# Combine softmax of all six chunks in one pass in the middle, running maximum as a logit column, w1 loads begun earlier, another memory order for w2

## The chip, the core and the metric

One core of a Trainium2 chip runs the whole program. Its engines are PE (TensorE: matmuls, with a separate stream PEld for weight loads), DVE (VectorE), ACT (ScalarE), POOL (GpSimd) and SP (SyncE, which here only issues DMAs). Each engine runs its instructions in the order in which the program has them, and waits for semaphores of the others. The metric is the device time of one execution in microseconds (us); the kernel before is timed three times and the median counts.

## The reference, cut to what matters

```python
# 1. gated recurrence per batch b (4) and head h (8), 768 tokens, head size 40
for t in range(S):
    m_new = maximum(f + m, i);  f_stab = exp(f + m - m_new);  i_stab = exp(i - m_new)
    C = f_stab * C + i_stab * outer(v, k);  n = f_stab * n + i_stab * k
    y[:, :, t] = sigmoid(o_gate) * (C @ q) / maximum(abs(n . q), 1)
x = y as 3072 tokens x 320
# 2. soft mixture of experts: 8 experts x 4 slots = 32 slots
logits = x @ phi                                   # 3072 x 32
d = softmax over the tokens of logits              # "dispatch", one maximum per slot
slot_input = d.T @ x                               # 32 x 320
for e in range(8): slot_out[e] = relu(slot_input[e] @ w1[e]) @ w2[e]
c = exp(logits - logits.max(1)); c /= c.sum(1) + 1e-9    # "combine", one maximum per token
x = c @ slot_out
# 3. h = x @ w_in; h * softmax(h), normalised, times g_ln, @ w_out   -> 3072 x 320
```

w_in and w_out arrive as 64-bit floats and are decoded on the chip.

## The kernel before

The work has three stages in one program.

**The recurrence.** A unit is 128 tokens of one batch, for all 8 heads: unit i = 4c + b is chunk c (of 6) of batch b (of 4). A loop runs over the 24 units; one pass of four units is called a cycle here. What a unit needs is a set of small closures, `ops(i)`, keyed by names, and the table `ORDER[i % 4]` gives the order in which the names are emitted: work of unit i (the output matmuls `o0` to `o3` into `po` and `pr`, the state updates `u0` to `u3` into `dps`), of unit i - 1 (`numa`, `numb`: DVE lines L296 and L298 build the numerator `num`; `den0` to `den2`: L306, L308, L310 the denominator `rd`; `sg`: L314; `x`: the product on POOL, L329, into a tile x; `C`: L325), of unit i - 2 (`xT`: the transpose of x) and of units i + 1 and i + 2 (`scA`, `scB` scores; `wA`, `wB`: DVE L253; `R`, `exp`: gate matrices). Since each engine keeps the order of emission, `ORDER` sets what stands behind what. `ENG` says which operations run on POOL; there, beside L329, run `cd` (L285), `kw` (L238) and `D4` (L457), a part of the decoding of w_in and w_out, which is spread over the loop too (DVE L446 to L455).

**Logits inside the loop.** Once per cycle the logits of a finished chunk g are made: `lt` multiplies phi by the four transposed x, so that `lt_t` has 4 batches x 32 slots on the 128 partitions and 128 tokens along the columns. For the dispatch softmax DVE takes the negated maximum per row (`tm0`, L360); `tm1` (L364) takes the minimum with that of the chunk before, which makes a running maximum; `tm2` exponentiates on ACT. `nt` and `ntc` (L379) bring the exponentials and the logits back to tokens on partitions, in the tile `dn` of 256 columns; `sl` and `acc` add up the slot inputs.

**The combine softmax, per chunk.** `row0` to `row7` run on the 128 logit columns of `dn`, spread over the cycle after: maximum (DVE L388), subtraction (POOL L390), exponential (ACT L392), sum (DVE L394), + 1e-9 (L396), reciprocal (L398), product (L400), two casts to the high part (L404), two subtractions for the low part (POOL L407). `cTp` (PE, four transposes) and `cTc` (ACT L430) put the result into `cT`. For the last chunk these steps run in the tail, all of those on DVE and POOL there on DVE.

**The middle.** After the loop follow the last unit's logits and sums, the slots' inputs `sbd`, then the expert layers: `w1_mm` (PE L761) in two column halves of 20 matmuls each, 512 columns wide (the trace shows two records for one such matmul); `hidden(0)` (ACT L754) and the four transposes `hT` (L766) of the first half stand ahead of the last 8 matmuls of the second. Then `cTp` of the last chunk, and `w2_mm` (L802) over the eight experts' w2 in the order 0, 2, 4, 6, 1, 3, 5, 7; then `soT`, `swc`, `sw_ps`, small steps that multiply the slots' output by w_in. `keep_warm` are matmuls whose result nobody uses.

**The last stage**, 24 tiles of 128 tokens through the layer of part 3, is a software pipeline with a table of its own.

**Loads.** SP issues every DMA in program order. A DMA also waits for the one that was issued eight before it, since there are eight semaphores. The 20 tiles of w1 (512 KB each) go one per unit from i = 4 to 22, the last at i = 22 too; the eight w2 (1280 KB each) follow, into memory that other tiles held, so that each waits for the last reader of these:

```python
W1_AT = 4
...
    for i in range(NU):
        ...
        if W1_AT <= i < W1_AT + 19:
            SP.dma_start(out=w1s[:, i - W1_AT, :], in_=w1p[i - W1_AT])
```

Of the kernel before, what the change touches and what calls it, by code (L numbers as in the profile page):

```python
# [45 lines left out]
def tile_kernel(  # L46
# [335 lines left out]
    def row_soft(g, k):  # L382
        nat = GR[g]["dn"][:, 128:256].rearrange("p (j s) -> p j s", j=NB)
        if k == 0:
            GR[g]["rs"] = rs_t
        rs = GR[g]["rs"]
        if k == 0:
            V.tensor_reduce(out=rs[:, 0, :], in_=nat, axis=AX.X, op=ALU.max)  # L388
# [640 lines left out]
```

## Time and profile before

| | us |
|---|---|
| times of three runs | 323.53, 321.88, 318.48 |
| median | 321.88 |
| the profiled execution | 319.83 |
| its span, first to last instruction | 318.0 |
| PE busy in the span | 297.0 |
| DVE busy | 253.1 |
| ACT busy | 213.8 |
| POOL busy | 74.5 |

The span is what the trace shows; 1.83 us of the profiled execution lie around it. Busy time of an engine holds time in which an instruction has begun and stands still, so that a busy engine need not be at its peak. By stages, the first logits' maximum (L360) starts at 51.2 us and the fifth at 147.2, the expert layers begin at 167.5, and the last stage runs from 194.9 to the end.

### The profile page before, as it was taken

To read this page: it belongs to the slowest core of one execution; us is meant where nothing else is said; L and a number is where in the kernel's file an instruction comes from. 1 tells how busy PE (TensorE), PEld (TensorE's weight loads), DVE (VectorE), ACT (ScalarE), POOL (GpSimd) and SP (SyncE) were. 2 spreads that over 40 slices of the span, in tenths; PEclk is the share of its full clock that TensorE was granted. 3 is DMA by queue.
4 is the path that set the end of the run, shared out by engine and by line. 5 is a ranking of instruction groups with operands and counts; after the bars stand their busy time and mean duration, and the time that the engine had idled before them with its cause. 6 is when DMAs were issued, how large, how long until landed. Compare 5 with 4: busy or idle time off the path is not lost.

```text
span 318.0 us, 8486 instructions
## 1 busy us (share of the span) xinstructions
PE 297.0 (93%) x3345; PEld 236.6 (74%) x3345; DVE 253.1 (80%) x568; ACT 213.8 (67%) x458; POOL 74.5 (23%) x107
## 2 busy tenths in 40 slices
PE   8985998999988998989999997999999999999995
PEld 5554676767766766767653335899999999999995
DVE  8688699899999999999827135988887787887841
ACT  5375676676666765857721604698988988988983
POOL 4412065465466365354300000000000000000000
PEclk9997899999999999999999999999999999999999
DMA  6961779788878798789999600011011010010111
GB/s 169 304 126 31 250 247 286 233 301 275 275 270 265 251 291 275 247 310 324 366 363 362 206 11 0 0 44 38 25 41 43 21 44 31 33 43 21 43 41 41
DMA packets 26086, 52.06 MB, mean 164 GB/s; under 512 B 3904, under 2 KB 15872, under 8 KB 26048
## 3 DMA queue, kind: packets, MB, share of 16 engines
q1 hardware_dynamic: 26048, 51.53, 50.3%
q8 instruction: 26, 0.43, 0.6%
q14 instruction: 12, 0.10, 0.1%
HBM read 47.03 MB, written 3.93 MB: 160 GB/s over the span
## 4 chain that ended last, share of the span: by engine, by line
PE 65%; DVE 19%; DMA 7%; ACT 3%; issue 3%; POOL 2%; POOLq 0%; DVEq 0%; ACTq 0%; SPq 0%
PE o L916 9%; PE o L918 9%; PE o L917 9%; PE uT L901 7%; PE h L857 4%; PE po L267 3%; PE sc L249 3%; DVE lb L253 3%; PE R L217 2%; PE R L218 2%; DMA w2s<-w 2%; DMA w1s<-w1p 2%; PE pr L270 2%; DMA gr<-m 2%; DVE kvo L314 2%
## 5 line engine op out<-in xcount | busy, mean ns | idle before, releaser
L916 PE MATMUL o<-wh,uh 128*128 128x320 f32 x192 | 62.9, 328 | 0.0
L918 PE MATMUL o<-wh,ul 128*128 128x320 f32 x192 | 59.1, 308 | 0.0
L917 PE MATMUL o<-wl,uh 128*128 128x320 f32 x192 | 59.0, 308 | 0.0
L876 DVE SCALAR_TENSOR_TENSOR u<-h,e 128x1024 f32<-128x1024 f32 (+1 forms) x25 | 29.4, 1181 | 16.8 <-ACT e L869 16.8
L267 PE MATMUL po<-kvo,lb 128*64 128x41 f32 x768 | 38.1, 230 | 3.3 <-PE sc L249 2.0
L267 PEld LDWEIGHTS po<-kvo,lb 128*64 128x64 f32 x768 | 30.7, 139 | 9.9 <-issue 4.8
L917 PEld LDWEIGHTS o<-wl,uh 128*128 128x128 f32 x192 | 36.2, 188 | 0.9
L916 PEld LDWEIGHTS o<-wh,uh 128*128 128x128 f32 x192 | 36.1, 188 | 0.9
L918 PEld LDWEIGHTS o<-wh,ul 128*128 128x128 f32 x192 | 36.0, 187 | 0.0
L909 DVE TENSOR_TENSOR ul<-uT,uh 128x512 fp32r<-128x512 f32 x48 | 33.0, 688 | 3.3 <-ACT uh L905 3.3
L253 DVE TENSOR_TENSOR lb<-sc,lb 128x512 f32<-128x512 f32 x48 | 31.2, 674 | 4.5 <-ACT lb L222 2.8
L905 ACT CAST uh<-uT 128x512 fp32r<-128x512 f32 x48 | 28.1, 585 | 9.9 <-PE uT L901 9.2
L249 PE MATMUL sc<-qk 64*128 64x128 f32 x384 | 34.2, 305 | 0.1
L249 PEld LDWEIGHTS sc<-qk 64*128 64x128 f32 x384 | 27.7, 202 | 7.8 <-issue 3.1
L901 PE MATMUL uT<-cst,u 128*128 128x128 f32 x192 | 28.8, 272 | 2.2 <-DVE u L876 2.2
L862 DVE TENSOR_REDUCE st<-h 128x1 f32<-128x1024 f32 x24 | 29.1, 1215 | 1.0 <-PE h L857 1.0
L869 ACT ACTIVATE e<-h,st 128x1024 f32<-128x1024 f32 (+1 forms) x25 | 26.7, 1069 | 4.3 <-DVE st L862 4.2
L230 ACT ACTIVATE kvo<-kvo 128x320 f32<-128x320 f32 x48 | 22.3, 469 | 10.5 <-DMA kvo<-kvo 10.2
L888 ACT ACTIVATE e<-u,st 128x1024 f32<-128x1024 f32 x24 | 27.7, 1153 | 1.8 <-DVE st L882 1.8
L222 ACT ACTIVATE lb<-R 128x1024 f32<-128x1024 f32 x24 | 24.3, 1012 | 6.8 <-PE R L218 6.8
L329 POOL TENSOR_TENSOR x<-num,kvo 128x320 f32<-128x320 f32 x23 | 18.7, 812 | 42.8 <-DVE kvo L314 26.9
L217 PE MATMUL R<-gr,gl 128*128 128x512 f32 x48 | 25.2, 582 | 1.7 <-DMA gr<-m 1.1
(229 smaller groups left out, 601.4 us busy)
## 6 DMA issues: line engine op xcount, KB each, us to landing
kvo<-kvo SPq DMA_DIRECT2D x24, 484.0 KB
w2s<-w SPq DMA_DIRECT2D x8, 1280.0 KB
w1s<-w1p SPq DMA_DIRECT2D x19, 512.0 KB
raw<-w SPq DMA_DIRECT2D x10, 512.0 KB
qk<-qkp SPq DMA_DIRECT2D x24, 160.0 KB
qk<-qkp SPq DMA_DIRECT2D x48, 80.0 KB
out<-ob SPq DMA_DIRECT2D x24, 160.0 KB
gt<-gates SPq DMA_DIRECT2D x1, 640.0 KB
```

The source lines that it names most:

```text
L217: PE.matmul(U[u]["R"][:, a], gl_t[c % 2][:, b, :], gr_t[c % 2][:, a * NR:(a + 1) * NR, :], start=True, stop=False)
L249: PE.matmul(U[u]["sc", a][:, r, :], t[p, 0, r, :], t[p, 1, r, :], start=True, stop=True)
L253: V.tensor_tensor(out=lb[:, a * NR:(a + 1) * NR, :], in0=U[u]["sc", a], in1=lb[:, a * NR:(a + 1) * NR, :], op=ALU.mult)
L267: PE.matmul(U[u]["po"][t, 2 * r + a, :], U[u]["lb"][:, a * NR + r, t], va(u, 2 * r + a), start=True, stop=True)
L862: V.tensor_reduce(out=F[i]["st"][:, 0:1], in_=F[i]["h"], axis=AX.XY, op=ALU.max, negate=True)
L876: V.scalar_tensor_tensor(out=F[i]["u"][:, c], in0=F[i]["h"].rearrange("p n f -> p (n f)")[:, c], scalar=1.0, in1=F[i]["e"][:, c], op0=ALU. ...
L901: PE.transpose(ps[:, k, :], F[i]["u"][:, (4 * n + k) * 128:(4 * n + k + 1) * 128], ident)
L905: A.copy(out=F[i]["uh"][:, 4 * n:4 * n + 4, :], in_=F[i]["uT", n])
L909: V.tensor_tensor(out=F[i]["ul"][:, c, :], in0=F[i]["uT", n], in1=F[i]["uh"][:, c, :].bitcast(F32), op=ALU.subtract)
L916: PE.matmul(o, uh, wh[:, k, :], start=k == 0, stop=False)
L917: PE.matmul(o, uh, wl[:, k, :], start=False, stop=False)
L918: PE.matmul(o, ul, wh[:, k, :], start=False, stop=k == FC - 1)
```

## The change

**One combine softmax.** The row operations leave the loop. `st_natural` copies the chunk's logits with tokens on partitions into its place in a new tile `nat` of 24 x 32 columns, which lives to the middle (the exponentials go into a `dn` of 128 columns). There `row_soft` runs once over 768 columns: maximum, subtraction, sum, + 1e-9, reciprocal and product on DVE, the exponential on ACT, six casts on ACT and six subtractions on POOL, 256 columns each. They are emitted between the two halves of `w1_mm`, ahead of `hidden(0)`, and the POOL part after `w1_mm`. The 24 transposes `cTp` and six copies `cTc` are spread over the middle, most of them where `keep_warm` stood. The tiles with the high and low parts share memory with the gate tiles gl and gr.

**Running maximum.** `lt_t` has a column more. The reduction L360 takes the maximum over 129 columns, of which the last is the maximum so far, and writes it back there; ACT negates it (`tm1`). The minimum L364 is gone.

**w1 loads.** Four are issued ahead of the loop, before the eight loads of gr; then units 3 to 17 load one each.

**Memory.** The five x tiles are allocated in two groups; w2 of expert 7 gets the place at the right end and h2 stands behind it, so that this load waits for other readers; `one_hot` and `swh` share a tile of the last stage's tag `u`.

```diff
 ORDER = (
...
-    "row0 D1b xT numa R C numb scA D3 D1 row1 scB o0 den0 sig0 cd den1 u3 D2 den2 row1.5 wA D4 row2 o3 u0 sig1 sg exp wB xTc u1 u2 row3 o1 o2 lraw x row4 sig2 kw right",
+ "D1b xT numa R C numb scA D3 D1 scB o0 den0 sig0 cd den1 u3 D2 den2 wA D4 o3 u0 sig1 sg exp wB xTc u1 u2 o1 o2 lraw x sig2 kw right",
...
-    lt_t = fixed("lt", [128, 128])
+    lt_t = fixed("lt", [128, T + 1])
...
     def tok_max(g, k):
+        top = lt_t[:, T:T + 1]
         if k == 0:
-            st = gst_t[g % 2]
-            GR[g]["st"] = st
-            V.tensor_reduce(out=st[:, 0:1], in_=GR[g]["lt"], axis=AX.X, op=ALU.max, negate=True)
+            GR[g]["st"] = gst_t[g % 2]
+            V.tensor_reduce(out=top, in_=lt_t[:, 0:T + (g > 0)], axis=AX.X, op=ALU.max)
         st = GR[g]["st"]
         if k == 1:
-            if g > 0:
-                V.tensor_tensor(out=st[:, 0:1], in0=st[:, 0:1], in1=mrun[0], op=ALU.min)
+            A.activation(out=st[:, 0:1], in_=top, func=AF.Copy, scale=-1.0)
...
     def st_natural(g):
-        A.copy(out=dn_t, in_=GR[g]["ntp"][:, 0:256])
-        GR[g]["dn"] = dn_t
...
+        A.copy(out=dn_t, in_=GR[g]["ntp"][:, 0:128])
+        A.copy(out=nat[:, NB * g:NB * g + NB].rearrange("p j s -> p (j s)"), in_=GR[g]["ntp"][:, 128:256])
...
+    def row_soft(k):
+        m, z = rs_t[:, 0, :], rs_t[:, 1, :]
...
+            V.tensor_reduce(out=m, in_=nat, axis=AX.X, op=ALU.max)
+            V.tensor_tensor(out=nat, in0=nat, in1=m.unsqueeze(2).to_broadcast([128, NU, NS]), op=ALU.subtract)
         elif k == 1:
...
             A.activation(out=nat, in_=nat, func=AF.Exp)
         elif k == 2:
...
+            V.tensor_reduce(out=z, in_=nat, axis=AX.X, op=ALU.add)
+            V.tensor_scalar(out=z, in0=z, scalar1=1e-9, scalar2=None, op0=ALU.add)
+            V.reciprocal(out=z, in_=z)
+            V.tensor_tensor(out=nat, in0=nat, in1=z.unsqueeze(2).to_broadcast([128, NU, NS]), op=ALU.mult)
         else:
...
+            for g in range(NC):
+                cs, x = cs_t[g], nat[:, 4 * g:4 * g + 4]
+                hi = cs[:, :, :, 0, :]
+                if k == 3:
+                    A.copy(out=hi, in_=x.unsqueeze(2).to_broadcast([128, 4, 2, NS]))
+                else:
+                    G.tensor_tensor(out=cs[:, :, :, 1, :], in0=x.unsqueeze(2).to_broadcast([128, 4, 2, NS]), in1=hi.bitcast(F32), op=ALU.subtract)
...
+    for n in range(4):
+        load_w1(n)
...
-        if W1_AT <= i < W1_AT + 19:
-            SP.dma_start(out=w1s[:, i - W1_AT, :], in_=w1p[i - W1_AT])
+        if 3 <= i < 18:
+            load_w1(i + 1)
...
     w1_mm(0, range(5))
+    for k in range(4):
+        row_soft(k)
     w1_mm(1, range(3))
     hidden(0)
     hT0 = hidden_T(0)
     w1_mm(1, range(3, 5))
+    row_soft(4)
...
+    w2s = {7: tl.tile([128, FC, DM], F32, tag="w2s7", name="w2s7")}
     h2 = tl.tile([128, FC, 4, 2, 8], F32, tag="h2", name="h2")
     G.memset(h2, 0.0)
...
-    keep_warm(2)
+    pe_cT(1)
...
+    st_cT(1)
+    pe_cT(2)
+    st_cT(2)
...
-    keep_warm(2)
+    for k in range(3, 5):
+        pe_cT(k)
+        st_cT(k)
...
-    keep_warm(2)
+    pe_cT(5)
+    st_cT(5)
```

On DVE, in the unit of which the trace shows 112 us, stood before (`rs` and `dn` are the combine softmax's, `cs` its high part, the others the unit's own work):

```order
L253 TENSOR_TENSOR lb_0_116<-sc_1_1192,lb_0_116 128x512
L396 TENSOR_SCALAR rs_91<-rs_91 128x4
L398 RECIPROCAL rs_91<-rs_91 128x4
L296 TENSOR_TENSOR num_104<-pr_1205,nat_100 128x328
L400 TENSOR_TENSOR dn_98<-dn_98,rs_91 128x128
L325 TENSOR_TENSOR C_111<-cd_118,dps 104x328
L404 CAST cs_99<-dn_98 128x4x32 x2
L298 TENSOR_TENSOR num_104<-num_104,po_1204 128x328
L306 SCALAR_TENSOR_TENSOR rd_103<-num_104 128x8
```

In the same place stands now:

```order
L254 TENSOR_TENSOR lb_0_124<-sc_1_1195,lb_0_124 128x512
L297 TENSOR_TENSOR num_112<-pr_1207,nat_108 128x328
L326 TENSOR_TENSOR C_119<-cd_126,dps 104x328
L299 TENSOR_TENSOR num_112<-num_112,po_1206 128x328
L307 SCALAR_TENSOR_TENSOR rd_111<-num_112 128x8
```

Four row operations (five instructions) are gone from between the unit's own, which keep their order. In the middle, ACT had this after the slots' inputs (`sbd`), up to the four activations of the experts' hidden layer:

```order
L725 COPY sbd<-siT_2385 64x4x4
L392 ACTIVATE dn_98<-dn_98 128x128
L754 ACTIVATE x_87<-so_ph_2308,fst 128x256 x2
L754 ACTIVATE acc<-ph_2411,fst 128x256
L754 ACTIVATE cst<-ph_2411,fst 128x256
```

ACT has now, in the same place (gl and gr are the memory of the high and low parts):

```order
L727 COPY sbd<-siT_2319 64x4x4
L391 ACTIVATE nat<-nat 128x768
L402 CAST gl_75<-nat 128x8x32
L402 CAST gl_76<-nat 128x8x32
L402 CAST gr_77<-nat 128x8x32 x2
L402 CAST gr_78<-nat 128x8x32 x2
L752 ACTIVATE x_92<-so_ph_2248,fst 128x256
L752 ACTIVATE x_93<-so_ph_2248,fst 128x256
```

The wide exponential and six casts stand ahead of the first two hidden activations, where one narrow exponential stood. On SP, ahead of the loop, the loads that follow g_ln's are now these, where the eight of gr stood directly behind it:

```order
L561 DMA gl<-g_ln 128x8x1
L436 DMA w1s<-w1p 128x1024 x4
L196 DMA gr_78<-m_130 8x128 x8
L440 DMA raw_94<-w 128x1024
L138 DMA qk_0_123<-qkp 40x1024
```

Four loads of w1 came in ahead of those of gr.

## Rows read from the trace of the kernel before

**Rows 1.** Busy time by stretch: us, busy of each engine (instructions), PEclk, DMA share, GB/s.

```profile
99.25:123.69 24.44, 22.99 (x412) 17.49 (x408) 23.71 (x56) 16.43 (x36) 12.88 (x18) 1.00 0.87 272
194.90:318.00 123.10, 117.56 (x822) 114.33 (x821) 95.29 (x195) 101.63 (x218) 0.00 (x0) 1.00 0.10 33
```

**Rows 2.** One line's instructions: duration ns min/median/max, first and last start.

```profile
L360 DVE TENSOR_REDUCE gst<-lt x5: 273/276/277, 51.2 to 147.2; 128x1 f32<-128x128 f32 x5
...
L364 DVE TENSOR_TENSOR gst<-gst,gst x4: 489/1370/1882, 76.1 to 147.8; 128x1 f32<-128x1 f32 x4
...
L388 DVE TENSOR_REDUCE rs<-dn x6: 269/272/277, 58.6 to 167.4; 128x4 f32<-128x128 f32 x6
```

**Rows 3.** Timeline of DVE from 98 us: start, us, instruction.

```profile
100.19 1.52 DVE L364 TENSOR_TENSOR gst<-gst,gst 128x1 f32<-128x1 f32 x1
```

**Rows 4.** Timeline of POOL, the same stretch.

```profile
99.74 1.26 POOL L457 TENSOR_TENSOR wo<-wo,dsc 128x512 f32<-128x512 f32 x1
100.97 0.72 POOL L238 TENSOR_TENSOR kvo<-kvo,nat 128x320 f32<-128x320 f32 x1
```

**Rows 5.** Timeline of DVE from 111 to 117 us.

```profile
112.25 0.45 DVE L396 TENSOR_SCALAR rs<-rs 128x4 f32<-128x4 f32 x1
...
112.84 0.49 DVE L296 TENSOR_TENSOR num<-pr,nat 128x328 f32<-128x328 f32 x1
113.24 0.28 DVE L400 TENSOR_TENSOR dn<-dn,rs 128x128 f32<-128x128 f32 x1
...
113.85 0.35 DVE L404 CAST cs<-dn 128x128 fp32r<-128x128 f32 x2
...
115.08 0.66 DVE L308 TENSOR_SCALAR rd<-rd 128x8 f32<-128x8 f32 x1
```

**Rows 6.** Timeline of POOL, the same stretch.

```profile
111.88 0.80 POOL L329 TENSOR_TENSOR x<-num,kvo 128x320 f32<-128x320 f32 x1 [0.49 <-DVE kvo L314]
...
114.14 0.87 POOL L407 TENSOR_TENSOR cs<-dn,cs 128x128 fp32r<-128x128 f32 x2 [0.77 <-DVE cs L404]
```

**Rows 7.** Costliest groups of the page: busy us, mean ns, idle before and its releaser.

```profile
L862 DVE TENSOR_REDUCE st<-h 128x1 f32<-128x1024 f32 x24 | 29.1, 1215 | 1.0 <-PE h L857 1.0
...
L888 ACT ACTIVATE e<-u,st 128x1024 f32<-128x1024 f32 x24 | 27.7, 1153 | 1.8 <-DVE st L882 1.8
...
L217 PE MATMUL R<-gr,gl 128*128 128x512 f32 x48 | 25.2, 582 | 1.7 <-DMA gr<-m 1.1
```

**Rows 8.** Timeline of DVE from 165 to 190 us.

```profile
167.77 0.16 DVE L741 RECIPROCAL fst<-fst 128x1 f32<-128x1 f32 x1
...
171.03 0.48 DVE L748 MEMSET so_ph<- 128x512 f32 x1
...
182.03 2.83 DVE L810 TENSOR_TENSOR wl<-wo,wh 128x2560 fp32r<-128x2560 f32 x1 [2.53 <-ACT wh L809]
```

**Rows 9.** Timeline of ACT, the same stretch.

```profile
172.09 0.84 ACT L754 ACTIVATE x<-so_ph,fst 128x256 f32<-128x256 f32 x2 [3.57 <-PE so_ph L761]
...
181.90 1.03 ACT L814 ACTIVATE one_hot<-cst 128x256 fp32r<-128x256 f32 x3
```

**Rows 10.** Timeline of PE, the same stretch.

```profile
174.45 0.66 PE L766 MATMUL hT<-cst,x 128*128 128x128 f32 x4
...
176.33 0.60 PE L761 MATMUL ph<-w1s,sbd 128*8 128x512 f32 x3
...
184.16 4.47 PE L802 MATMUL so_ph<-w2s,h 128*8 128x320 f32 x58 [0.52 <-DMA w2s<-w]
```

**Rows 11.** Timeline of SP's issues, from 20 us and from 140 us.

```profile
24.66 5.00 SPq L195 DMA_DIRECT2D gr<-m  x8
...
146.11 31.86 SPq L796 DMA_DIRECT2D w2s<-w  x8
```

**Rows 12.** Busy time by stretch, columns as in rows 1, near the start.

```profile
26.00:28.00 2.00, 0.00 (x0) 0.00 (x0) 1.97 (x4) 1.15 (x4) 0.38 (x1) 0.86 0.04 11
28.00:30.00 2.00, 1.51 (x9) 1.19 (x11) 1.93 (x7) 1.98 (x5) 1.13 (x2) 0.50 0.03 6
```

More of the change, by code (lines that the diff above doesn't have):

```diff
@@ L88, in tile_kernel @@
     eyeb = cpool.tile([128, 128], BF16, tag="eyeb", name="eyeb")
+    nat = cpool.tile([128, NU, NS], F32, tag="nat", name="nat")
+    gl_t = [cpool.tile([128, NB, T], F32R, tag=f"gl{n}", name=f"gl{n}") for n in range(2)]
+    gr_t = [cpool.tile([128, NH, T], F32R, tag=f"gr{n}", name=f"gr{n}") for n in range(2)]
     w1_ctx = ExitStack()
@@ L384, in row_soft @@
+    cs_t = []
+    for x in (gl_t[0], gl_t[1], gr_t[0], gr_t[1]):
+        cs_t += [x[:, 4 * h:4 * h + 4].rearrange("p u (q k s) -> p u q k s", q=2, s=NS) for h in range(x.shape[1] // 4)]
+    def row_soft(k):
+        m, z = rs_t[:, 0, :], rs_t[:, 1, :]
         if k == 0:
[L385 to L388, printed above, removed]
+            V.tensor_reduce(out=m, in_=nat, axis=AX.X, op=ALU.max)
+            V.tensor_tensor(out=nat, in0=nat, in1=m.unsqueeze(2).to_broadcast([128, NU, NS]), op=ALU.subtract)
@@ L422, in pe_cT, with load_w1 @@
     def pe_cT(g):
-        ps = ps_o.tile([128, 512], F32, tag="misc", name=f"cTp{g}")
-        cs = GR[g]["cs"]
+        if g in (2, 3):
+            if g == 2:
+                GT["cT"] = ps_sc.tile([128, 2, 512], F32, tag="R", name="cTp23")
+            ps = GT["cT"][:, g - 2]
+        else:
+            pool, tag = {0: (ps_o, "misc"), 1: (ps_sc, "s1"), 4: (ps_sc, "s0"), 5: (ps_sc, "s1")}[g]
+            ps = pool.tile([128, 512], F32, tag=tag, name=f"cTp{g}")
         for j in range(NB):
-            PE.transpose(ps[:, 128 * j:128 * j + 128], cs[:, j].rearrange("p a b s -> p (a b s)").bitcast(F32), ident)
+            PE.transpose(ps[:, 128 * j:128 * j + 128], cs_t[g][:, j].rearrange("p q k s -> p (q k s)").bitcast(F32), ident)
         GR[g]["cTp"] = ps
     def st_cT(g):
-        A.copy(out=cT[:, 4 * g:4 * g + 4, :].rearrange("p j t -> p (j t)"), in_=GR[g]["cTp"])
+        out, in_ = cT[:, 4 * g:4 * g + 4, :].rearrange("p j t -> p (j t)"), GR[g]["cTp"]
+        A.copy(out=out, in_=in_)
+    def load_w1(n):
+        SP.dma_start(out=w1s[:, n, :], in_=w1p[n])
     def load_raw(n):
@@ L558, in tile_kernel @@
     st_sig(0)
-    G.memset(x_all[:, :, DM:384], 0.0)
-    G.memset(x_all[:, :, DM:DM + 1], 1.0)
+    for x in x_t:
+        G.memset(x[:, DM + 1:384], 0.0)
+        G.memset(x[:, DM:DM + 1], 1.0)
     def ops(i):
@@ L624, in ops @@
                 T[f"tm{k}"] = lambda k=k: tok_max(g, k)
-            for k in (0, 1, 1.5, 2, 3, 4, 5, 5.5, 6, 7):
-                T[f"row{k}"] = lambda k=k: row_soft(g, k)
             T["lt"] = lambda: pe_logit(g)
@@ L632, in ops @@
             T["acc"] = lambda: st_acc(g)
-            T["cTp"] = lambda: pe_cT(g)
-            T["cTc"] = lambda: st_cT(g)
         return T
@@ L645, in tile_kernel @@
         T_ = ops(i)
-        for t in ORDER[i % NB].split() + ([] if i < NU - 1 else ["row5", "row5.5", "row6", "row7"]):
+        for t in ORDER[i % NB].split():
             if t in T_:
@@ L693, in tile_kernel @@
     A.activation(out=st[:, 2:3], in_=mrun[0], func=AF.Exp, scale=-1.0, bias=st[:, 0:1])
-    A.copy(out=lt_t, in_=lt)
+    A.copy(out=lt_t[:, 0:T], in_=lt)
     mfin = bank("pr", "mfin")
@@ L703, in tile_kernel @@
     PE.transpose(dT[:, 0:128], d_t, ident)
-    A.copy(out=dn_t[:, 0:128], in_=dT[:, 0:128])
+    A.copy(out=dn_t, in_=dT[:, 0:128])
     keep_warm()
@@ L715, in tile_kernel @@
     ltT = bank("misc", "ltT")
-    PE.transpose(ltT[:, 0:128], lt_t, ident)
-    A.copy(out=dn_t[:, 128:256], in_=ltT[:, 0:128])
-    GR[g]["dn"] = dn_t
+    PE.transpose(ltT[:, 0:128], lt_t[:, 0:T], ident)
+    A.copy(out=nat[:, NB * g:NU].rearrange("p j s -> p (j s)"), in_=ltT[:, 0:128])
     wm = wo_mean([6, 7])
```

63 lines of the change are left out of this document (19 added, 44 removed), and 6 rows, old and new, of the table ORDER.

## The prediction

> **What bounds the kernel now.** I read the busy time by stretch first, then the timelines of DVE, POOL, ACT and PE around each edit. In a cycle of the recurrence the reader is to see DVE busy 23.71 of 24.44 us, PE 22.99, at full granted clock, and the DMA engines at 0.87 [rows 1]. So DVE sets the cycle, with PE half a microsecond to a microsecond behind it. The starts of L360 give four cycles in 96.0 us, 24.0 each [rows 2]. The last stage takes 123.1 us, 117.56 of them PE [rows 1]; the diff leaves it alone, and I cost it at nothing. So the sum has three parts: what DVE gains in the loop, what the middle pays, and what the loads do.
>
> **The row operations leave the loop.** Per cycle DVE loses two reductions, one of 0.27 us [rows 2] and one like it, L396 with 0.45, a reciprocal, L400 with 0.28 and two casts in 0.35 [rows 5]: 1.62 without the reciprocal. Not all of it pays. L296 writes `num`, which POOL's L329 still reads until 111.88 + 0.80 = 112.68, and L296 starts at 112.84 [rows 5, 6]: L396 and the reciprocal stand in a time in which DVE would wait for POOL, so they pay nothing. Behind L296 nothing covers: L400 is 0.28 and the casts 0.35, each less the 0.09 by which neighbours overlap (L296 runs to 113.33, L400 starts at 113.24 [rows 5]), together 0.45. Then there is L308: 0.66 us for 8 columns, where the reduction of 128 columns takes 0.27, while POOL runs the two subtractions L407, 0.87 us from 114.14 on, and the `cd` behind them [rows 2, 5, 6]. Without L407 that stall shrinks or goes; bounds 0 and 0.66 - 0.17 = 0.49 (0.17 taken as for a one-column reciprocal, 0.16 [rows 8]); with what L306 loses I take 0.55. Of the two reductions, 0.54, I take two thirds, 0.37, since DVE sits at the front of the cycle nearly everywhere but not at each wait. Sum 0.45 + 0.55 + 0.37 = 1.4 us per cycle, in four cycles **5.6 us** (bounds 3 and 8). POOL and ACT lose work too, but neither bounds the cycle (12.88 and 16.43 of 24.44 [rows 1]). PE loses four transposes per cycle, off the bound.
>
> **The minimum L364.** It moves one column, and takes 0.49 to 1.88 us, 5.1 in its four places [rows 2]. The one at 100.19 ends at 101.71, as POOL's back-to-back L457 (from 99.74) and L238 (to 100.97 + 0.72 = 101.69) end [rows 3, 4]. So it doesn't compute, it stands until POOL has a pause. Taken out, DVE goes on to L298 and L325, which are as wide as L296 and so cost 0.4 us each with their overlap [rows 5], and then to L306, which reads two operands from SBUF as L364 did, still ahead of POOL's pause: 0.6 to 0.8 of the 1.52 is gained and the rest of the stall passes to L306. I take that share, 0.4, everywhere: 5.1 x 0.4 = **2.0 us** (bounds 0.5 and 5.1).
> The Trainium skill, "SBUF — State Buffer", section on who interferes with whom, says that a DVE instruction with two SBUF inputs and a GpSimd instruction that reads SBUF lock each other out for a whole instruction. The end of L364 with L238 agrees [rows 3, 4]. By that rule the stall is passed on to the next such instruction of DVE, and removing one instruction doesn't remove it.
> In its place L363 on ACT copies one column, about 0.26 us, with ACT busy 16.43 of 24.44 [rows 1]; behind it in ACT's queue stands a copy of x, for which PE has slack. Nothing. Were ACT late, the exponential of the logits would be, and with it `nt` on PE, 0.3 us per cycle.
>
> **Loads in the loop.** The bytes per cycle stay; 272 GB/s over 24.44 us [rows 1] make 6.65 MB, in 22.5 us 295 GB/s, at a share of 0.87 x 24.44 / 22.5 = 0.94. Transfers land later against the work. PE has waited 1.1 us for gr in all [rows 7]; bounds for what is added are 0 and twice that, and I take **0.7 us** as a loss. In the last cycles w1 no longer stands ahead of qk and kvo; I have not counted a gain.
>
> **The prologue.** The eight gr go out from 24.66 on, 5.0 us [rows 11]; between 26 and 28 us the DMA engines run at 0.04 [rows 12]. Four w1 are 2.1 MB, which at 300 GB/s (about the loop's rate) fill 7 us of that lull. Their four issues fit ahead of 24.66; but the last four gr now wait for the landing of the four w1, and raw and qk behind them. PE needs gr some 2 us after the last issue. Bounds -0.5 and +1.5; I take **+0.3 us**. More memsets of x tiles on POOL stand there under DMA waits: nothing.
>
> **The middle.** The combine softmax now has 768 columns. A reduction costs between 0.27 at 128 [rows 2] and 1.215 at 1024 [rows 7], linear 0.94; the subtraction and the product between 0.28 at 128 [rows 5] and 2.83 at 2560 [rows 8], 0.95; the exponential below 1.153 at 1024 [rows 7], 0.9. DVE is free after L741, 167.93, and two memsets of 0.48 [rows 8], at 168.9. Then 0.94 + 0.95 + 0.9 + 0.94 + 0.35 (the two small ones) + 0.95, and 0.15 for two hand-overs, end at 174.1. The six casts on ACT, at three in 1.03 [rows 9], end at 176.2. Before, `hidden(0)` ran at 172.09 to 172.93 [rows 9], covered by PE's work, and `hT` started at 174.45 [rows 10]. Now its two activations run from 176.2 to 177.0, `hT` goes from 176.65 on to 177.3, and the rest of `w1_mm`, which took from 175.04 to 176.93 (the last start 176.33 + 0.60), ends at 179.2: **2.2 us** later, after a wait of PE of as much.
> The load of w2 of expert 7 is the last of the eight; its issue ended at 146.11 + 31.86 = 177.97 and PE had it at 184.16, after a wait of 0.52 [rows 10, 11]. It waited for `cTp`, which it no longer does; now the last `w1_mm` releases it, at 179.2 + 0.1: 1.7 later than the start of the old issue, 177.6, and so at 185.9. PE's first half of `w2_mm` comes 2.2 later and ends at the same 185.9, so the second half starts **1.7 us** later, the 0.52 of waiting being eaten. Behind it stand four transposes of `cT(2)` which replace no `keep_warm`, at most the 0.66 of four transposes [rows 10]; I take 0.4. The other `cTp` stand where `keep_warm` stood, and their copies on ACT beside PE's work: nothing. Sum **2.1 us** (bounds 0.5, if the chain is as fast as its parts overlap, and 4.5, if a POOL subtraction holds up h2's memset and each hand-over costs 0.5).
>
> **Sum.** 5.6 + 2.0 - 0.7 - 0.3 - 2.1 = 4.5 us. The profiled execution took 319.83 (span 318.0 and 1.83 around it), so its like would be 315.3. The ratio 0.986 on the median of 321.88 gives **317.4 us**. Two per cent, about what a measurement here can tell from no change, are 6.4 us.
>
> **Rivals.**
> 1. *The stalls vanish with their instructions.* Then each removed duration pays: 1.62 x 4 + 5.1 = 11.6, less 2.1 and 0.3, gives 9.2, and 321.88 x 310.6 / 319.83 = 312.6 us. For it: DVE is busy 0.97 of the cycle. Against: L364 ends with POOL's chain, which stays, and L396 stands under POOL's L329.
> 2. *PE takes over.* It is busy 22.99 in the cycle [rows 1]; if its order allows no less than 23.2, four cycles give 4 x 0.8 = 3.2 and the loads take their 0.7: with the middle that is 0, 321.8 us. For it: its busy time; against: part of this is PE's own standing still, and its four transposes leave.
> 3. *The wait in the tail costs clock: slower.* Between 26 and 28 us PE did nothing, the granted clock fell to 0.86 of that stretch and stood at 0.50, the lower level of 1.2 GHz, in the next [rows 12]. The place now is the wait for `hidden(0)`, 174.5 to 176.7, 2.2 us, after full work. If the chain takes 1 us more, and the clock falls for the rest of `w1_mm` and the first half of `w2_mm`, 1.9 + 4.4 us of work take twice as long, about +6 with what hides behind the w2 load: 4.5 - 1 - 6 = -2.5, 324.4 us. Slower than before it is from a gain in the loop below 9.4; with rival 2's loop it would be 329.
> The Trainium skill, "TensorE: Matmul & The Clock Gate", Part 1, says that the array falls to its lower clock when it has idled, which is this case; the row agrees [rows 12], and by it the forecast would hold only if PE's wait stays as short as I make it.
> 4. *The early loads of w1 push gr back* beyond +1.5: the gate matrix R of the second chunk waits. At worst gr lands when the 2.1 MB have, near 29 us, 4.3 after its first issue at 24.66 [rows 11] and 2.8 more than I count: 320.2 us.
>
> **How the numbers follow.** The forecast 0.52, rival 1 0.20, rival 2 0.14, rival 3 0.09, rival 4 0.05. The forecast's own bounds make it 312 to 321, with about a quarter of it below 315.4, where faster by 2% begins: 0.20 + 0.13 = 0.33, and a little more since rivals 1 and the forecast lie close: 0.35 faster. Slower by 2% is rival 3 with a weak loop: 0.07. The rest, 0.58, is within 2%. The range 310.5 to 322.5 leaves the low tail of rival 1 and most of rival 3 out.
>
> **What the profile of the changed kernel would show.** Starts of L360 22.2 to 22.6 us apart; stalls of over 0.5 us on the `rd` instructions at 100 us where L364 was; PE without work for 2 to 2.5 us ahead of `hT`, with granted clock 1.00 after it; w2_mm's second half 1.7 us later against the end of `sbd`; the last stage 123 us as before. Wrong it is if the cycle falls below 21.5 or stays above 23.5, if the clock shows 0.5 behind the wait, or if the loop begins more than 1 us later than now.

## The result, and the profile after

The changed kernel takes 320.93 us, the median of 20 runs (318.94 to 325.68); the kernel before, in 20 runs beside it, 319.15 (316.75 to 323.53). The ratio is 1.0087, 95% interval 1.0061 to 1.0113: slower by 0.9%, where 317.4 us and a gain were forecast. The ratios here leave out, on either side, executions over 1.5% above the fastest of their kernel, so that they differ a little from those of the medians (1.0056 here). Its profiled execution took 322.54 us with a span of 320.7, so 2.7 more span than the kernel before.

Where the 2.7 us come from is told by five sections of the span, read from the starts of L360, of the first expert matmul and of the first matmul of the last stage (at 194.1 us before; [rows 1] count it from 194.9):

| section | before, us | after, us | difference |
|---|---|---|---|
| start to the first L360 | 51.2 | 50.5 | -0.7 |
| four cycles | 96.0 | 93.4 | -2.6 |
| to the first expert matmul | 20.3 | 20.2 | -0.1 |
| the middle, to the last stage | 26.7 | 31.4 | +4.7 |
| last stage | 123.9 | 125.2 | +1.3 |

The four cycles and the last stage of the changed kernel, busy time by stretch, columns as in rows 1:

```profile
50.51:74.42 23.91, 21.68 (x387) 16.45 (x387) 20.65 (x47) 15.82 (x34) 11.41 (x15) 1.00 0.80 251
74.42:98.16 23.74, 21.78 (x391) 16.57 (x387) 20.18 (x47) 16.14 (x35) 11.65 (x15) 1.00 0.92 291
98.16:121.09 22.93, 21.50 (x368) 16.17 (x366) 21.92 (x47) 15.58 (x35) 11.74 (x15) 1.00 0.91 282
121.09:143.94 22.85, 21.33 (x379) 16.06 (x376) 20.86 (x46) 14.97 (x31) 11.22 (x14) 1.00 0.77 221
...
195.49:320.70 125.21, 119.71 (x825) 116.23 (x824) 95.71 (x195) 102.72 (x220) 0.00 (x0) 0.98 0.10 32
```

[rows 1] had DVE busy 23.71 of 24.44 us. Now DVE has 20.18 to 21.92 of 22.85 to 23.91: by its busy time it no longer sets the cycle, and neither does PE, which keeps 1.4 to 2.2 us free in each. The work that was taken out is gone, but the cycle has shrunk by 0.65 us, where 1.4 to 1.8 were forecast. The last stage shows 0.98 of granted clock where it had 1.00. From the page of the kernel before, the shares of the chain that ended last, by engine:

```profile
PE 65%; DVE 19%; DMA 7%; ACT 3%; issue 3%; POOL 2%; POOLq 0%; DVEq 0%; ACTq 0%; SPq 0%
```

The same from the page of the changed kernel, then by line, and the group of L218, the old L217:

```profile
PE 53%; DMA 21%; DVE 15%; issue 3%; ACT 3%; SPq 2%; POOL 1%; DVEq 0%; ACTq 0%; POOLq 0%
DMA w1s<-w1p 11%; PE o L928 9%; PE o L926 9%; PE o L927 9%; PE uT L911 7%; DMA gr<-m 6%; PE h L867 4%; DMA raw<-w 2%; DMA w2s<-w 2%; PE po L268 2%; PE R L218 2%; PE so_ph L805 1%; DVE lb L254 1%; PE R L219 1%; PE lt_last L681 1%
...
L218 PE MATMUL R<-gr,gl 128*128 128x512 f32 x48 | 24.9, 568 | 6.0 <-DMA gr<-m 4.2
```

DMA has 21% of the chain, where it had 7%, and PE waits 4.2 us for gr where it waited 1.1 [rows 7]. One piece of that chain, in order of time: start, us, what.

```profile
83.49 6.15 DMA w1s<-w1p
...
89.66 6.47 DMA w1s<-w1p
...
96.15 4.59 DMA gr<-m
...
101.02 0.47 PE R L218
```

Two loads of w1, one after the other, then one of gr, 4 KB, which takes 4.59 us, then R on PE. SP issues a load when the load eight before it has landed: the second w1 is issued 0.02 us after the first has landed, and this gr 0.02 us after the second. So w1, w1 and gr hang on each other.

In the middle, ACT's timeline (start, us, instruction) and PE's:

```profile
171.63 1.32 ACT L402 CAST gr<-nat 128x256 fp32r<-128x256 f32 x4
172.98 0.84 ACT L752 ACTIVATE x<-so_ph,fst 128x256 f32<-128x256 f32 x2
```

```profile
173.51 1.11 PE L764 MATMUL hT<-cst,x 128*128 128x128 f32 x4 [2.33 <-ACT x L752]
174.55 2.51 PE L759 MATMUL ph<-w1s,sbd 128*8 128x512 f32 x11
...
176.89 0.60 PE L759 MATMUL ph<-w1s,sbd 128*8 128x512 f32 x3
...
185.02 4.47 PE L805 MATMUL so_ph<-w2s,h 128*8 128x320 f32 x58 [1.28 <-DMA w2s<-w]
```

The casts end at 172.95 and the two hidden activations at 173.82; PE had waited 2.33 us for them. The trace then shows `hT` at 1.11 us for 0.66 before, and the eleven records at 2.51 for 1.47: PE runs at its lower clock. `w1_mm` ends at 177.49, 13.36 after the first expert matmul, where it was 9.47 [rows 10]. The granted clock in two places, columns as in rows 1:

```profile
172.00:174.00 2.00, 0.49 (x3) 0.42 (x4) 1.72 (x1) 1.79 (x6) 2.00 (x4) 0.82 0.06 21
174.00:176.00 2.00, 2.00 (x11) 0.49 (x14) 0.00 (x0) 0.00 (x0) 2.00 (x4) 0.50 0.00 0
198.00:200.00 2.00, 0.20 (x2) 0.21 (x3) 1.62 (x4) 2.00 (x6) 0.00 (x0) 1.00 0.00 0
200.00:202.00 2.00, 1.96 (x10) 1.65 (x9) 2.00 (x5) 1.14 (x4) 0.00 (x0) 0.65 0.00 0
202.00:204.00 2.00, 2.00 (x7) 1.67 (x7) 1.69 (x3) 0.47 (x2) 0.00 (x0) 0.50 0.00 0
```

Behind the wait at 171.2 to 173.5 the clock goes to 0.50, which is 1.2 GHz. Behind a wait of 2.18 us at 197.6 to 199.8 in the last stage it does so again; the kernel before has the same wait, from 196.2 to 198.4, and its granted clock stays at 1.00:

```profile
198.00:200.00 2.00, 1.59 (x10) 1.11 (x10) 2.00 (x5) 1.58 (x4) 0.00 (x0) 1.00 0.00 0
200.00:202.00 2.00, 1.89 (x13) 1.68 (x13) 2.00 (x5) 0.42 (x2) 0.00 (x0) 1.00 0.00 0
```

### The profile page after: what moved, and what is told of

Same layout as the page of the kernel before. It is cut to its first block, busy times and chain, and to the rows that moved or that the text cites. A ratio compares the mean times of both kernels' runs of the same rounds, so it can differ in the third digit from the quotient of the medians.

```text
span 320.7 us, 8424 instructions
## 1 busy us (share of the span) xinstructions
PE 295.6 (92%) x3333; PEld 235.0 (73%) x3333; DVE 245.0 (76%) x525; ACT 217.6 (68%) x469; POOL 72.8 (23%) x106
## 4 chain that ended last, share of the span: by engine, by line
PE 53%; DMA 21%; DVE 15%; issue 3%; ACT 3%; SPq 2%; POOL 1%; DVEq 0%; ACTq 0%; POOLq 0%
DMA w1s<-w1p 11%; PE o L928 9%; PE o L926 9%; PE o L927 9%; PE uT L911 7%; DMA gr<-m 6%; PE h L867 4%; DMA raw<-w 2%; DMA w2s<-w 2%; PE po L268 2%; PE R L218 2%; PE so_ph L805 1%; DVE lb L254 1%; PE R L219 1%; PE lt_last L681 1%
## 5 line engine op out<-in xcount | busy, mean ns | idle before, releaser
L254 DVE TENSOR_TENSOR lb<-sc,lb 128x512 f32<-128x512 f32 x48 | 31.2, 674 | 4.0 <-ACT lb L223 2.6
L250 PE MATMUL sc<-qk 64*128 64x128 f32 x384 | 32.3, 295 | 1.1 <-DMA qk<-qkp 1.1
L250 PEld LDWEIGHTS sc<-qk 64*128 64x128 f32 x384 | 26.3, 194 | 8.4 <-issue 4.1
L218 PE MATMUL R<-gr,gl 128*128 128x512 f32 x48 | 24.9, 568 | 6.0 <-DMA gr<-m 4.2
L879 ACT ACTIVATE e<-h,st 128x1024 f32<-128x1024 f32 (+1 forms) x25 | 26.7, 1069 | 3.7 <-DVE st L872 3.6
L898 ACT ACTIVATE e<-u,st 128x1024 f32<-128x1024 f32 x24 | 27.7, 1155 | 0.3 <-DVE st L892 0.2
L911 PEld LDWEIGHTS uT<-cst,u 128*128 128x128 f32 x192 | 24.0, 141 | 3.1 <-DVE u L886 2.4
```

Source lines behind the costliest of these rows:

```text
L218: PE.matmul(U[u]["R"][:, a], gl_t[c % 2][:, b, :], gr_t[c % 2][:, a * NR:(a + 1) * NR, :], start=True, stop=False)
L250: PE.matmul(U[u]["sc", a][:, r, :], t[p, 0, r, :], t[p, 1, r, :], start=True, stop=True)
L254: V.tensor_tensor(out=lb[:, a * NR:(a + 1) * NR, :], in0=U[u]["sc", a], in1=lb[:, a * NR:(a + 1) * NR, :], op=ALU.mult)
L911: PE.transpose(ps[:, k, :], F[i]["u"][:, (4 * n + k) * 128:(4 * n + k + 1) * 128], ident)
```

## Experiments

Ratios are to the kernel before, run beside each; the three sections are those of one profiled execution each. "Cycles" are the four from the first to the fifth L360, "middle" is from the first expert matmul to the last stage. Before: 96.0 and 26.7; changed: 93.4 and 31.4.

| experiment | cycles | middle | last stage | ratio, 95% interval |
|---|---|---|---|---|
| e1 hidden first | 89.7 | 27.6 | 124.0 | 0.9957, 0.9920 to 0.9994 |
| e2 wait filled | 91.7 | 29.6 | 125.2 | 1.0014, 0.9975 to 1.0053 |
| e3 w1 as before | 93.5 | 31.2 | 123.9 | 1.0043, 1.0005 to 1.0081 |
| e4 four w1 tiles | 86.6 | 30.1 | 125.2 | one run, 312.32 us |
| e5 w1 behind gr | 90.6 | 30.2 | 125.3 | 1.0067, 1.0029 to 1.0105 |
| e6 only the column | 93.1 | 26.5 | 123.9 | 0.9920, 0.9880 to 0.9960 |
| e7 e1, other w2 order | 91.5 | 28.7 | 123.9 | 1.0004, 0.9971 to 1.0036 |
| e8 before, four w1 tiles | 94.1 | 26.5 | 125.1 | one run, 317.37 us |
| e9 e1, w1 spread | 87.9 | 26.6 | 124.0 | 0.9872, 0.9815 to 0.9929 |
| e10 e9, last wait filled | 88.4 | 27.7 | 123.9 | 0.9865, 0.9822 to 0.9907 |
| e11 changed, w1 spread | 88.8 | 30.1 | 125.2 | 0.9929, 0.9896 to 0.9962 |
| e12 before, column, w1 spread | 92.5 | 26.5 | 123.9 | 0.9877, 0.9824 to 0.9929 |

The changed kernel, e1, e2 and e7 have the same loop, and their cycles are 93.4, 89.7, 91.7 and 91.5: 91.6 on the mean, 4.4 under before. So the profile of the changed kernel was one of the slower ones there, and a difference of 2 us between the loops of two profiles tells little by itself. PE's wait for gr within the four cycles goes along with them: 4.2 us in the changed kernel, 2.4 in e2 and e7, 0.3 in e1.

**e1, the hidden activations ahead of the casts.**

```diff
     w1_mm(0, range(5))
-    for k in range(4):
+    for k in range(2):
         row_soft(k)
+    hidden(0)
+    for k in range(2, 4):
+        row_soft(k)
     w1_mm(1, range(3))
-    hidden(0)
     hT0 = hidden_T(0)
...
-    row_soft(4)
+    row_soft(4, (0,))
...
     G.memset(h2, 0.0)
+    row_soft(4, range(1, NC))
```

> The changed kernel, with the first two hidden activations ahead of the six casts in ACT's queue, and with five of the six POOL subtractions behind the memset of h2. Theory T (the tail): PE's 2.33 us of waiting ahead of hT goes, and with it the 1.5 us that hT and the rest of w1_mm lost at half clock; from the start of the expert layers to the last stage 27.0 to 27.5 us instead of 31.4, and the last stage keeps its clock, 123.9 instead of 125.2. Ratio to the kernel before 0.986 to 0.992. Rival (the load of w2 of expert 7 binds the tail): PE waits for this load instead, the stretch stays above 29 us, ratio over 1.0.

PE's timeline:

```profile
169.59 0.66 PE L764 MATMUL hT<-cst,x 128*128 128x128 f32 x4
...
179.76 4.47 PE L808 MATMUL so_ph<-w2s,h 128*8 128x320 f32 x58 [1.43 <-DMA w2s<-w]
...
190.22 0.77 PE L870 MATMUL h<-swf,cT 128*128 128x512 f32 x2
```

PE no longer waits ahead of `hT`, which takes 0.66 again, and the middle is 27.6 us: 3.7 of the 4.7 are back, by the order on ACT and the five subtractions together, which this run does not tell apart. What is left, 0.9, is about the wait for w2 of expert 7, 1.43 where it was 0.52 [rows 10], and the four transposes of `cT(2)`. The ratio is 0.9957 and not under 0.992 as expected: the loop is that of the changed kernel, and the short one of this profile (315.98 us, the fastest of 12 executions with a median of 318.48) is not typical of it.

**e2, the wait filled with unused matmuls.**

```diff
     hidden(0)
+    keep_warm(14)
     hT0 = hidden_T(0)
```

> The changed kernel, with 14 unused matmuls of 128 columns ahead of hT, which fill PE's wait there and change nothing else. Theory T: the clock stays at its upper level, hT and the rest of w1_mm take 2.5 us instead of 4.0; the wait of 2.3 stays as it is; the stretch of the tail shrinks by 0.8 to 1.5 us (the load of w2 of expert 7 is released earlier by as much), ratio 1.002 to 1.005. Rival: the clock at that place is no cause, the stretch stays at 31.4 us, ratio 1.009.

PE's timeline:

```profile
174.29 0.60 PE L764 MATMUL hT<-cst,x 128*128 128x128 f32 x4
174.82 1.47 PE L759 MATMUL ph<-w1s,sbd 128*8 128x512 f32 x11
...
193.65 0.77 PE L868 MATMUL h<-swf,cT 128*128 128x512 f32 x2
```

`hT` begins 10.22 us after the first expert matmul, 0.84 later than in the changed kernel since the 14 take longer than the wait, and yet `w1_mm` ends at 12.65, 0.7 sooner: at the upper clock. The middle falls by 1.8 us, more than the 1.5 expected: PE also no longer waits for w2 of expert 7, 1.28 us in the changed kernel. The clock is a cost of its own there. That the 14 matmuls kept it is not shown: in e4, e5 and e11, below, it held behind the same wait without them.

**e3, w1 loaded as before.**

```diff
-    for n in range(4):
-        load_w1(n)
...
-        if 3 <= i < 18:
-            load_w1(i + 1)
+        if 4 <= i < 23:
+            load_w1(i - 4)
```

> The changed kernel, with the loads of w1 where the kernel before had them (none ahead of the loop, units 4 to 22 one each). Theory L (the loads bind the loop, w1 and gr standing in each other's way wherever a unit has both): four cycles stay at 93 to 95 us, the first L360 within 0.7 us of 50.5, and qk of the last units comes later. Rival (the early loads have disturbed the order of the queue): the four cycles fall to 88 to 90 us, ratio under 0.997.

The cycles are 93.5 (L360 at 52.49 and at 145.98), as in the changed kernel's profile; the first L360 came 2.0 us later than there, where 0.7 was expected. So no run shows that starting w1 in the prologue is the cause of the loss or, by itself, a gain.

**e4 and e8, 15 loads of w1 taken out of the loop,** in the changed kernel, whose other four stand ahead of the loop, and in the kernel before, where units 4 to 7 keep them. Both multiply by four tiles of w1, and the last, over and over, in place of twenty.

```diff
-        if 3 <= i < 18:
-            load_w1(i + 1)
...
-                w = w1s[:, ti, 512 * n:512 * n + 512] if ti < 19 else w1l[:, 512 * n:512 * n + 512]
+                w = w1s[:, ti % 4, 512 * n:512 * n + 512] if ti < 19 else w1l[:, 512 * n:512 * n + 512]
```

(In e8: `W1_AT <= i < W1_AT + 4` and the same line of `w1_mm`.)

> The changed kernel, without the 15 loads of w1 in the loop: the expert layers multiply by the first four tiles (and the last) of w1 again and again, so that the loop has 0.5 MB less to load per unit. Theory L: the waits of PE for gr vanish and the four cycles fall from 93.4 to 87 to 90 us, which is what the DVE work that was taken out allows. Rival (PE's own order, or DVE with POOL, caps the cycle at some 23.3 us): the four cycles stay above 92 us.

> The kernel before, with four loads of w1 in the loop instead of 19 (the expert layers multiply by these four tiles, and the last, again and again). If DVE sets the cycle of the kernel before and the loads don't, as I read its profile, the four cycles stay at 94.5 to 96.5 us, while the changed kernel fell from 93.4 to 86.6 by the same cut. Rival (the loads already cost the kernel before as much): the four cycles fall to 91 us or less.

Two cycles of e4 and the sum of all four:

```profile
70.28:92.02 21.74, 21.54 (x391) 16.47 (x387) 20.93 (x47) 15.92 (x35) 11.64 (x15) 1.00 0.73 203
92.02:114.07 22.05, 21.69 (x391) 16.58 (x388) 21.24 (x48) 15.94 (x35) 11.62 (x15) 1.00 0.65 201
...
sum 86.64, PE 85.05 PEld 64.78 DVE 83.34 ACT 61.97 POOL 45.76; mean PE 21.26 PEld 16.20 DVE 20.84 ACT 15.49 POOL 11.44
```

The same of e8:

```profile
73.51:97.22 23.71, 22.50 (x400) 17.03 (x393) 23.22 (x55) 16.32 (x35) 13.02 (x18) 1.00 0.66 188
97.22:120.96 23.74, 22.53 (x400) 17.06 (x394) 23.25 (x56) 16.32 (x35) 13.04 (x18) 1.00 0.63 188
...
sum 94.08, PE 88.87 PEld 66.88 DVE 91.37 ACT 63.77 POOL 51.35; mean PE 22.22 PEld 16.72 DVE 22.84 ACT 15.94 POOL 12.84
```

Taking out 15 loads gives the changed kernel 6.8 us (93.4 to 86.6; 5.0 from the mean of 91.6) and the kernel before 1.9 (96.0 to 94.1), each a little more than expected. The loads hold up the one; the other is, by its busy time, held by DVE, 91.37 of 94.08. Without these loads the change is worth 94.08 - 86.64 = 7.4 us in the loop, from one profile each. PE is then busy 85.05 of 86.64.

**e5, w1 issued behind the unit's gr.**

```diff
-        if 3 <= i < 18:
-            load_w1(i + 1)
...
             if t in T_:
                 T_[t]()
+        if 3 <= i < 18:
+            load_w1(i + 1)
```

> The changed kernel, with a unit's load of w1 issued behind its two loads of gr (4 KB each), where it stood ahead of them; the bytes stay. Theory L1 (gr lands late because it queues behind w1): PE's waits for gr, 4.2 us in the changed kernel's profile, go under 1.5, the four cycles fall from 93.4 to 88 to 90 us, ratio to the kernel before 0.990 to 0.998. Rival L2 (it is the amount of loads, in whatever order): the four cycles stay at 90 to 93.5 us, the waits move to qk, kvo or raw, ratio 1.003 to 1.009.

PE's waits, in total, times, longest:

```profile
PE sc L250 <- DMA qk<-qkp: 2.3, 3, 0.9
```

gr is gone from PE's longest waits (0.8 us in the whole execution, as L1 had it) and qk has come in, 0.9 of its 2.3 us within the four cycles. Yet the cycles are 90.6, between those of the same loop in the old order, and the ratio is 1.0067, both as L2 had it. So PE's wait for gr is where the loads' cost shows in the changed kernel, but a better place for gr does not bring the time back.

**e6, only the column.** The kernel before, with `tok_max`, `lt_t` and `st_logit` as in the change.

> The kernel before, with the running maximum as column 128 of the logits and nothing else changed: L364 is gone, ACT negates. My prediction's step: 2.0 us of the 5.1 that L364 shows come off, the rest of the stall passes to the next instruction of DVE; the four cycles 94.0 us, ratio 0.992 to 0.996. Rival 1: the whole 5.1 comes off, ratio 0.984 to 0.988. Rival 2 (the loads or PE hold the cycle there): under 0.7 us, ratio 0.998 to 1.001.

```profile
L359 DVE TENSOR_REDUCE lt<-lt x5: 274/276/278, 50.1 to 143.1; 128x1 f32<-128x129 f32 x4, 128x1 f32<-128x128 f32 x1
```

Cycles 93.1 (50.07 to 143.15), 2.9 less, and a ratio of 0.992: 2.6 us of 319, with 1.3 to 3.8 in its interval. My step said 2.0 of 5.1. In the changed kernel, at the place where L364 stood, DVE's timeline shows the instruction that stands now, and POOL's the one that lets it go:

```profile
99.70 0.96 DVE L307 SCALAR_TENSOR_TENSOR rd<-num 128x8 f32<-128x8 f32 x1
```

```profile
99.89 0.74 POOL L239 TENSOR_TENSOR kvo<-kvo,nat 128x320 f32<-128x320 f32 x1
```

L307, 8 columns wide, takes 0.96 us, to 100.66, as POOL's L239 ends at 100.63. The stall passed on, less what L299 and L326 ran meanwhile. The Trainium skill, "SBUF — State Buffer", section on who interferes with whom, has a DVE instruction with two SBUF inputs and a GpSimd instruction that reads SBUF shut each other out; the trace agrees, 0.96 us here for 0.17 elsewhere.

**e7, w2 of expert 7 multiplied last.**

```diff
-    w2_mm(1, range(FC))
+    w2_mm(1, range(FC), range(3))
+    w2_mm(1, range(FC), (3,))
```

> The first experiment's kernel, with the matmuls of the second half of w2_mm in another order: all of experts 1, 3 and 5 ahead of those of expert 7, whose load comes last. If PE's wait of 1.4 us there is the load of expert 7's w2 alone, it goes under 0.3, the stretch from the start of the expert layers to the last stage falls from 27.6 to 26.2 us, and the ratio to 0.989 to 0.994. Rival: the wait is for another thing and stays, ratio 0.996.

The expectation fell. PE shows no wait there, but the middle is 28.7 us, 1.1 more than in e1. Records of this line by stretch (us, PE busy and count, PEld busy and count, PEclk, DMA):

```profile
180.00:182.00 2.00, 2.00 (x31) 0.74 (x23) 1.00 0.00 0
182.00:184.00 2.00, 2.00 (x12) 0.70 (x8) 1.00 0.00 0
```

With three experts in turn 31 records begin in 2 us, one each 0.065 us, with expert 7 alone 12, one each 0.17 us. Each is 0.43 us long either way; those of different experts write different strips of 32 partitions, those of one expert the same strip. So the order that took the wait away cost more than the wait.

**e9, e1 with w1 spread over the loop.**

```diff
-        if 3 <= i < 18:
-            load_w1(i + 1)
+        if 3 <= i < 23 and i % NB != 1:
+            load_w1(4 + sum(k % NB != 1 for k in range(3, i)))
```

> The first experiment's kernel (hidden activations ahead of the casts), with the 15 loads of w1 spread over units 3 to 22, none in every fourth unit, where units 3 to 17 had one each. In the changed kernel the DMA engines' share is 0.92 and 0.91 in the second and third cycle and 0.77 in the fourth. Theory L2 (the amount of loads per time caps the loop): the shares level out, the four cycles fall from 89.7 to 93.4 us (four profiles of this loop) to 88 to 90 us, ratio to the kernel before 0.985 to 0.992. Rival (the cap lies in the chain through eight semaphores, not in the rate): the four cycles stay at 90 to 93 us, ratio 0.993 to 0.999.

Two cycles and the sum of four, columns as in rows 1; then PE in the middle:

```profile
71.44:93.08 21.64, 21.44 (x387) 16.39 (x387) 20.85 (x48) 15.75 (x35) 11.62 (x15) 1.00 0.85 278
...
115.53:136.94 21.41, 20.32 (x351) 15.27 (x352) 20.40 (x47) 14.50 (x30) 11.41 (x14) 1.00 0.91 287
sum 87.93, PE 85.38 PEld 65.01 DVE 83.12 ACT 61.80 POOL 46.35; mean PE 21.34 PEld 16.25 DVE 20.78 ACT 15.45 POOL 11.59
```

```profile
164.38 0.66 PE L764 MATMUL hT<-cst,x 128*128 128x128 f32 x4
...
173.47 4.47 PE L808 MATMUL so_ph<-w2s,h 128*8 128x320 f32 x58 [0.36 <-DMA w2s<-w]
...
183.94 0.77 PE L870 MATMUL h<-swf,cT 128*128 128x512 f32 x2
```

The DMA share is 0.84 to 0.91 in all four cycles; with w1 in units 3 to 17 it was 0.92 and then 0.77. The cycles are 87.9, the middle 26.6 with 0.36 us of waiting for w2, the ratio 0.9872. PE is busy 21.44 of 21.64: by its busy time it sets the cycle now, and its wait for gr is gone. This execution was the fastest of its six (309.71 us, median 313.47); e10 has the same loop and 88.4. With e10 and e12 this is the fastest kernel of the study, 1.3% ahead of before and 2.1% of the changed one.

It does not tell L2 from its rival, though: with no w1 in every fourth unit the chain through eight semaphores has less to carry too. And a high share does not by itself make a long cycle. In the profile of e7, with the loop of the changed kernel, the second cycle is

```profile
73.97:96.00 22.03, 21.74 (x389) 16.52 (x387) 20.93 (x48) 16.04 (x35) 11.63 (x15) 1.00 0.93 289
```

22.03 us at 0.93, where the changed kernel's profile had 23.74 at 0.92. When the loads are issued counts, but whether by rate or by the chain stays open.

**e10, also the last stage's wait filled.**

```diff
-u0:0 u1:0 w:2 T0:0
+u0:0 u1:0 w:12 T0:0
```

> The kernel of the experiment beside it, with ten more unused matmuls of 128 columns in PE's wait of 2.2 us ahead of the last stage's first transposes. In the profiles so far the clock fell behind this wait in some runs (the changed kernel, the second, fourth, fifth and eighth experiment) and not in others, for 1.35 us where it fell. If it is this wait, the last stage takes 123.9 us with the clock at its upper level, and the ratio is 0.000 to 0.004 lower than beside it. Rival: the clock there depends on what went before, and the ten matmuls delay the transposes: the last stage stays at 124 to 125.2 us, ratio the same or higher.

The group of the transposes uT: busy, mean ns of one, idle before:

```profile
L914 PE MATMUL uT<-cst,u 128*128 128x128 f32 x192 | 28.8, 272 | 0.0
```

The idle time is 0.0 where it was 2.2, the last stage 123.9 us, the ratio 0.9865 against 0.9872. But e9 kept its clock there too, so these two don't tell whether the ten matmuls are what keeps it. The middle was 27.7 us, with 1.48 us of waiting for w2 of expert 7 where e9 had 0.36.

**e11, the changed kernel with only w1 spread.**

> The changed kernel, with only the loads of w1 spread over units 3 to 22; the tail is as the change has it. If the two causes add (loads in the loop, PE's wait and its clock in the tail), the four cycles take 87.5 to 89.5 us and the tail 29.5 to 31.4, ratio to the kernel before 0.997 to 1.003, about 1.3% above the kernel with both cured (0.9872). Rival (what the loop gains is lost again at the w2 loads, which then come later against it): ratio above 1.005.

PE's timeline in the middle:

```profile
170.30 0.80 PE L764 MATMUL hT<-cst,x 128*128 128x128 f32 x4 [2.33 <-ACT x L752]
171.03 1.47 PE L759 MATMUL ph<-w1s,sbd 128*8 128x512 f32 x11
...
190.97 0.78 PE L867 MATMUL h<-swf,cT 128*128 128x512 f32 x2
```

Cycles 88.8 and middle 30.1, both as expected; in this profile the clock behind the wait of 2.33 us held but for `hT` itself (0.80). The ratio, 0.9929, is below the range that I gave, which was too high for what these two would add up to: against 96.0 and 26.7 they make 3.8 us less, 0.988, and 0.992 with the last stage's 1.3. Spreading 15 loads turns the change from 0.9% slower into 0.7% faster.

**e12, the kernel before with the column and w1 spread,** the softmax still per chunk in the loop.

> The kernel before, with the running maximum as a column, and w1 loaded as in the ninth experiment: four ahead of the loop, 15 spread over units 3 to 22. The combine softmax stays in the loop, per chunk. If the softmax in the loop costs DVE what I made it (5.6 us in four cycles, less 2 to 3 in the middle), the four cycles stay at 92 to 93.5 us since DVE sets them, ratio 0.989 to 0.994, above that of the ninth experiment. Rival (the spread of the loads was all): the four cycles fall to 90 us or less, ratio 0.980 to 0.988, and the softmax could have stayed.

A cycle and the sum of four:

```profile
73.90:96.91 23.01, 22.44 (x400) 17.04 (x393) 22.47 (x55) 16.42 (x36) 12.87 (x18) 1.00 0.85 261
...
sum 92.48, PE 89.35 PEld 67.32 DVE 88.82 ACT 63.62 POOL 50.93; mean PE 22.34 PEld 16.83 DVE 22.21 ACT 15.91 POOL 12.73
```

The cycles are 92.5, as expected, with DVE busy 22.47 of 23.01. But the ratio, 0.9877, lies below the range expected and in that of the rival. In the profiles e9 and e10 are 4.5 and 4.1 us faster than this in the loop, and 0.1 and 1.2 slower in the middle. In the times they are not: 0.9877 here, 0.9872 and 0.9865 there, six runs each, with intervals of 0.4 to 0.6% to either side, not beside each other on one chip. Whether the softmax in the middle is worth anything over the column and the spread is not settled here.

## Why the prediction was wrong

**The step that failed is "Loads in the loop".** I took 0.7 us, with 2.2 as the upper bound, from PE's one wait of 1.1. That wait was short while DVE was the slower one, so it told nothing of what the loads would allow. The price is the gap between the loop with its loads and without: 93.4 - 86.6 = 6.8 us in the profile of the changed kernel, 91.6 - 86.6 = 5.0 on the mean of its loop. e8 shows that the kernel before paid 1.9 of that already (one profile each), so the term that I put at 0.7 measured 4.9 in the one profile and 3.1 on the mean. The spread of the same loads (e9, e10, e11) brings back most of it: cycles of 87.9 to 88.8. What I had in hand was the share of 0.87, and I worked out 0.94 for the faster cycle, and stopped there; but a share alone would not have given the price either (22.03 us at 0.93 in e7). How the loads hold the loop up, by their rate or by the chain of issues, stays open. Rival 2 had the size of the loop right, 92.8 us for 93.4, and the place wrong: not PE's order took over, but the loads.

**The row operations and the minimum were about right.** 5.6 + 2.0 = 7.6 us were forecast; the loops without the loads differ by 7.4, one profile each. For L364 alone 2.0 were forecast and 2.6 (by the times) to 2.9 (by the profile) measured, and the rest of its stall is where I put it. For the row operations alone the loops of e9 and e10 against e12 give 4.1 to 4.6, for 5.6. One stall I had not foreseen: the product `sg`, L314, takes 9.8 us of DVE in the four cycles of e8, and as L315 11.3 in e4, so that some of what the others lost was passed on to it.

**The middle was mis-sized: 2.1 against 4.7.** The chain itself came as worked out: PE's wait was 2.33 us, 2.2 forecast. Two terms were missing or too small. Rival 3, the clock, at 0.09, happened: 1.4 us in the changed kernel and in e3 (`w1_mm` ends 13.36 and 13.38 after the start), not in e4, e5 and e11 (12.01 and 12.02), with the same wait in all five. The forecast had named the clock at 0.50 behind the wait as a sign of being wrong, and it came. My price of 6 was too high, since the lower clock lasted only for `hT` and the rest of `w1_mm`. And the second half of `w2_mm` began 2.9 us later even without it (19.58 in e11 against 16.69), where I had 1.7: PE got w2 of expert 7 some 7 us after its issue ended, 6.2 before. In e1 the wait for it was 1.43, in e9, with the same middle, 0.36, so this load's time varies by a microsecond; why, no run shows.

**The prologue shows no cost.** The first L360 came at 50.5, for 51.2 before, and between 48.4 and 52.7 in the experiments, without a relation to where w1 is loaded; 0.3 can't be told within this.

**The last stage,** which I costed at nothing, lost 1.3 us in six of the thirteen profiles that have its wait of 2.2 us, and none in the others. Five of the six are among the six whose `hT` stands behind the casts (the changed kernel, e2, e4, e5 and e11, not e3); of the seven with the middle of before or of e1 only e8 fell, the kernel before with fewer loads. So the loss may well hang on the longer middle, though the diff leaves the stage alone; one profile each doesn't show it, and no run tells how.

**The sum.** Loop -4.4 on the mean, middle +3.4 to +4.7, and 1.3 more where the last stage's clock falls: -1.0 to +1.6, where the medians say +1.8 and the ratio +2.8. What is missing is within the spread of the loop and of the start, which differ by 3.7 and 4.3 us between profiles; no run accounts for it.

## What to carry to other kernels

When an engine that is busy 0.97 of a loop is relieved, price the next limit from what it would allow by itself, not from how long anyone waits for it now: a short wait for loads says only that something else was slower. One run with the loads taken out of both kernels gives that number; here it was 86.6 against 94.1 us, and it showed both that the work taken out was priced about rightly and that the loads ate much of it. Loads that nobody needs soon are then to be spread evenly over the loop: here three in four units in place of one in each, 1.6% from the changed kernel to e11. And work that is moved to a quiet place should go behind what the busiest engine waits for there: six casts ahead of two activations, with the subtractions ahead of h2's memset, cost the middle up to 3.7 us, 1.4 of them by the clock.
